# Seven products for batch 0's hidden layer, and four column strips for a pair's sums

## The chip, the cores and the metric

The kernel runs on one core of one Trainium2 chip. The metric is the time of one execution on the device in microseconds (us). The engines are named as the profile names them: PE is TensorE (PEld its weight loads, which overlap its products), DVE is VectorE, ACT is ScalarE, POOL is GpSimd and SP is SyncE, which here only issues transfers. Each engine works through its own list of instructions in order; they meet through semaphores.

## The reference, cut to what matters

Two blocks, one after the other, in float32. First an attention in which a query sees a key only if both fall in the same bucket of a six-bit hash; then a Fourier mixing block with a two-layer network.

```
B, H, S, D = 4, 8, 768, 64            # attention; DM = H*D = 512
mask   = bucket(q @ proj)[:, None] == bucket(k @ proj)[None, :]
scores = where(mask, q @ k.T / sqrt(D), -1e9)
attn   = exp(scores - max) / (sum + 1e-9)
x      = attn @ v                      # (B, S, DM)

mixed  = real(fft(fft(x, axis=1), axis=2))
u      = x + mixed
un     = (u - mean(u)) / sqrt(var(u) + 1e-6)
out    = u + relu(un @ w_ch1) @ w_ch2  # w_ch1: 512 x 2048, w_ch2: 2048 x 512
```

The two weights arrive as float64, and the kernel turns them into float32 on the chip.

## The kernel before, in words

**Attention.** A batch has four pairs of heads (`NPAIR`), numbered n = 4b + t. A pair is worked through in six key chunks of 128 keys (`NT`). `weigh` computes scores for the chunk (PE, line L869, and L862 for the five pairs 0 to 4, whose hash mask is added by a product), ACT takes the exponential (L873), and for the later pairs DVE applies the mask (L879, two instructions per chunk). DVE adds the chunk's weights to `acc` (L957). `values` multiplies the weights with v one chunk later (L890, tiles `oo`). The queue `pending` holds that later part. At the end of a pair, `scale` forms the sums of the weights over the keys by multiplying `acc` with ones (L910), writes them into two banks (one for each half of the queries), turns each by a DVE transpose (L914), adds a small number (L917), takes the reciprocal (L918), spreads it by a transpose back (L919) and multiplies x by it (L923). The ones are 64 columns wide, so that head h fills the partitions 64h to 64h+63. Two other products already write four strips of 32 partitions into one bank: the hash bits of pairs 5 to 15 (L804) and the weights' column sums in `average` (L656).

**Mixing.** `fold` and the tiles `cs`, `A`, `B` (L1007 to L1090) do the Fourier transforms as products with tables. The layer norm's mean is taken out of the weights beforehand (`average`, `centre`), and its factor is applied at the end. The hidden layer is `mlp0` for batch 0 and `mlp7` for batches 1 to 3. `mlp0` is the plain form: 16 blocks of 128 hidden units, two halves of the 768 columns, four products over the 512 inputs (L1314), 128 products of 128x128 with 384 columns in all, and one relu by ACT for each tile (L1318). `mlp7` takes two by two blocks with seven products instead of eight (Strassen's scheme in Winograd's form): per f of `HF` = 8 it issues 14 products (L1361), 112 in all, but has to add and subtract blocks: on the weights' side four combinations per f (`quarters`, L1149 to L1152, tile `tq`), which `mlp0` computes once beside its own work and writes to a scratch tensor `ad` in HBM with the plain blocks (L1154, L1155), on x's side four differences t1 to t4, and on the results' side five DVE additions (L1387, L1394, L1399, L1403, L1411), six ACT copies out of the product banks and four relus per f. The batches 1 to 3 read the blocks back from `ad` through a ring of 12 buffers. `outer7` is the second layer, in seven products for all batches (L1232); it is entered twice, once for each half of the hidden units, since the second weight's seven blocks for one half fill `w2` (tiles `right7`).

**The second weight's arrival.** `weights2` fetches 16 slices of w_ch2 as float64 through raw buffers in the tile `z` (L685, issued on POOL), and `narrow` converts each: DVE L631, L635 and L644 (twice), ACT L639, L646, L647. A slice can be fetched only when the slice that had its buffer has been converted. Three buffers are used. After each second slice, DVE forms four combinations (L1198 to L1201). The first eight slices are converted from the A and B steps of batch 0's mixing on, the other eight beside the second half of its hidden layer.

**Order.** The first attention, batch 0's, has an order written by hand for all engines (`manual_schedule`). From then on the mixing of batch b - 1 is interleaved with the attention of batch b: a loop draws steps of `mix` at an even rate over the 24 key chunks, counted by `MIX`, and a scheduler puts the instructions of each engine in order. The last mixing stands alone. Line numbers here are those of this kernel.

## Time and profile before

| | |
|---|---|
| median of 6 runs | 1111.39 us (1108.37 to 1113.9) |
| the profiled execution | 1111.44 us; span from first to last instruction 1109.7 us |
| PE busy | 1064.7 us of the span (96%) |
| DVE busy | 778.2 us (70%) |
| ACT busy | 455.9 us (41%) |
| batch 0's attention | 0 to 138 us |
| batch 1's attention with batch 0's mixing | 138 to 425 us |
| batch 2's attention with batch 1's mixing | 425 to 684 us |
| batch 3's attention with batch 2's mixing | 684 to 935 us |
| batch 3's mixing | 935 to 1110 us |

The bounds of the stages are the starts of each batch's `cs` products in the chain of waits. The stage of batch 0's mixing is the longest: 287 us, where the next has 259. A PE product in float32 is recorded as two instructions, so the counts of PE rows are twice the products. A PE row's busy time is the union of overlapping records; the mean of one is longer than its share.

### The profile page before, as it was taken

Reading aid. Unit: us, or ns where it says so; the run is one execution under the profiler, and the core shown is the slowest. Engines: PE = TensorE matmul, PEld = TensorE weight load, DVE = VectorE, ACT = ScalarE, POOL = GpSimd, SP = SyncE. Lnnn points to the kernel's source line nnn. Section 1 sums busy time; section 2 is a strip of 40 time slices with the busy share of each in tenths; the row PEclk is TensorE's granted clock in tenths of the full one; section 3 lists DMA queues with packets and bytes.
Section 4 is the critical chain, followed back from the end, with each engine's and each line's share of the span. In section 5 each row is a group of like instructions: output and inputs, shape, how many; then the busy total and the mean of one; then the engine's idle time right before and its main releaser. Section 6 shows DMA issues by size and latency. Waiting matters only on the chain.

```text
span 1109.7 us, 13908 instructions
## 1 busy us (share of the span) xinstructions
PE 1064.7 (96%) x4925; PEld 652.4 (59%) x4925; DVE 778.2 (70%) x1298; ACT 455.9 (41%) x879; POOL 79.2 (7%) x141
## 2 busy tenths in 40 slices
PE   7999987999999999999999999999999999999996
PEld 3334353555855676555664567545674569768675
DVE  5889968739598686975767796984866885644353
ACT  6778545525064224454325422355224422341420
POOL 1000000002110020030000011021000002100000
PEclk9999998999999999999999999999999999999998
DMA  9744444521057043222144234213032205122401
GB/s 228 200 95 114 82 152 118 209 46 27 1 141 226 22 116 123 48 67 77 29 152 91 67 67 166 37 45 94 17 114 67 76 29 171 48 87 77 132 19 41
DMA packets 175566, 103.13 MB, mean 93 GB/s; under 512 B 129408, under 2 KB 162816, under 8 KB 175488
## 3 DMA queue, kind: packets, MB, share of 16 engines
q1 hardware_dynamic: 168400, 83.93, 28.3%
q0 software_dynamic: 5520, 17.83, 5.1%
q8 instruction: 41, 0.67, 0.2%
q10 hardware_dynamic: 1568, 0.39, 0.2%
q14 instruction: 37, 0.30, 0.1%
HBM read 81.14 MB, written 20.97 MB: 92 GB/s over the span
## 4 chain that ended last, share of the span: by engine, by line
PE 68%; DVE 19%; DMA 4%; ACT 4%; issue 2%; SPq 1%; DVEq 0%; ACTq 0%
PE o L1232 23%; PE h_p L1361 18%; PE sc L869 7%; PE oo L890 6%; PE h L1314 6%; DVE acc L957 4%; DVE pk L879 3%; DMA zraw<-in_moe_w_ch_dram 3%; PE cs L1047 2%; PE sum L910 2%; PE A L1076 1%; ACT pk L873 1%; PE B L1076 1%; DMA ad<-tq 1%; DVE x L1090 1%
## 5 line engine op out<-in xcount | busy, mean ns | idle before, releaser
L1232 PE MATMUL o<-w,h 128*128 128x256 f32 x1152 | 258.9, 381 | 0.1
L1232 PEld LDWEIGHTS o<-w,h 128*128 128x128 f32 x1152 | 216.7, 190 | 42.6 <-issue 4.7
L873 ACT ACTIVATE pk<-sc 128x768 f32<-128x768 f32 x192 | 148.0, 808 | 89.9 <-PE sc L869 59.9
L879 DVE SCALAR_TENSOR_TENSOR pk<-qb,kb,pk 128x768 f32<-128x768 bf16 x132 | 128.5, 1011 | 62.2 <-ACT pk L873 61.5
L869 PE MATMUL sc<-qt,kt 64*128 64x384 f32 x768 | 154.6, 506 | 3.8 <-ACT pk L873 3.8
L890 PE MATMUL oo<-pk,vn 128*64 128x385 f32 (+1 forms) x768 | 151.8, 504 | 2.8 <-ACT x L903 2.5
L1361 PE MATMUL h_p<-x,w 128*128 128x384 f32 x384 | 139.0, 493 | 1.4 <-ACT h L1402 1.4
L1361 PE MATMUL h_p<-w 128*128 128x384 f32 x288 | 106.0, 491 | 0.7 <-ACT u L1103 0.7
L957 DVE TENSOR_TENSOR acc<-acc,pk 128x1536 f32<-128x1536 f32 (+1 forms) x72 | 105.6, 1480 | 0.6
L1361 PEld LDWEIGHTS h_p<-x,w 128*128 128x128 f32 x384 | 70.4, 190 | 57.7 <-ACT h L1402 5.1
L890 PEld LDWEIGHTS oo<-pk,vn 128*64 128x64 f32 x768 | 49.1, 137 | 93.7 <-issue 73.6
L869 PEld LDWEIGHTS sc<-qt,kt 64*128 64x128 f32 x768 | 67.0, 188 | 51.0 <-issue 25.4
L1314 PE MATMUL h<-x,w 128*128 128x384 f32 x256 | 86.2, 491 | 1.4 <-ACT h L1318 1.4
L1361 PEld LDWEIGHTS h_p<-w 128*128 128x128 f32 x288 | 53.3, 190 | 41.0 <-ACT w L1410 3.3
L1314 PEld LDWEIGHTS h<-x,w 128*128 128x128 f32 x256 | 47.6, 190 | 37.8 <-ACT h L1318 2.9
L1262 ACT COPY tq<-o 128x256 f32<-128x256 f32 x24 | 8.9, 372 | 115.4 <-PE o L1232 115.4
L1244 DVE SCALAR_TENSOR_TENSOR w<-o,rs,w 128x256 f32<-128x256 f32 x56 | 26.7, 478 | 40.8 <-PE o L1232 40.7
L1232 PE MATMUL o<-w 128*128 128x256 f32 x192 | 46.1, 383 | 4.0 <-DVE w L1244 2.4
L985 POOL DMA_DIRECT2D out_dram<-w x30 | 16.3, 546 | 428.0 <-issue 309.1
L1232 PEld LDWEIGHTS o<-w 128*128 128x128 f32 x192 | 35.9, 190 | 11.4 <-DVE w L1244 4.5
L1251 ACT COPY tq<-o 128x256 f32<-128x256 f32 x24 | 8.9, 370 | 74.6 <-PE o L1232 74.6
L1278 DVE TENSOR_TENSOR tq<-tq,o 128x256 f32<-128x256 f32 x24 | 10.1, 421 | 38.2 <-PE o L1232 38.2
(161 smaller groups left out, 1266.6 us busy)
## 6 DMA issues: line engine op xcount, KB each, us to landing
w<-ad SPq DMA_DIRECT2D x168, 128.0 KB, 2.0
w<-bd SPq DMA_DIRECT2D x42, 512.0 KB, 4.6
zraw<-in_moe_w_ch_dram POOLq DMA_DIRECT2D x21, 512.0 KB, 4.5
bd<-w SPq DMA_DIRECT2D x14, 512.0 KB, 4.9
vn<-in_v_dram SPq DMA_DIRECT2D x32, 192.0 KB, 3.5
qn<-in_q_dram SPq DMA_DIRECT2D x120, 48.0 KB, 2.3
kn<-in_k_dram SPq DMA_DIRECT2D x60, 96.0 KB, 3.3
ad<-tq SPq DMA_DIRECT2D x8, 512.0 KB, 4.1
```

Of the source, the lines that this page charges most:

```text
L869: last[0] = nc.tensor.matmul(ps[:, h, 0:HALF], kt[rows, ks], qt[rows, qs], start=kb is not None, stop=True,)
L873: nc.scalar.activation(pk[:, g, :, 0:HALF], ps[:, :, 0:HALF], AF.Exp, scale=SCALE)
L879: nc.vector.scalar_tensor_tensor(w, qb[:, h].rearrange("p (g s) -> p g s", g=2), kb[:, h, c : c + 1], w, op0=ALU.is_equal, op1=ALU.mult,)
L890: nc.tensor.matmul(oos[g][h * D : (h + 1) * D, 0:w], nat["v", n][:, (2 * c + h) * D : (2 * c + h + 1) * D], pk[:, g, h, 0:w], start=(c == ...
L910: nc.tensor.matmul(ps[h * D : (h + 1) * D, :], ones, part[:, g, h], start=(i == 0), stop=(i == len(sums) - 1),)
L957: nc.vector.tensor_tensor(acc[:, g], (first if c == 1 else acc)[:, g], new[:, g], op=ALU.add,)
L1047: nc.tensor.matmul(ps[:, pc + 2 * lo : pc + 2 * hi - 1 : 2], z[:, cp, pc, par, t * P : (t + 1) * P], ch[:, cp, pc, lo:hi], start=(cp == 0) ...
L1076: nc.tensor.matmul(ps[:, cols], F[:, par, k, t, j * P : (j + 1) * P], sq[:, t, k, cols], start=(t == 0), stop=(t == 1),)
L1232: nc.tensor.matmul(ps, a[:, r], right7[i][:, r], start=start and r == 0, stop=r == HF // 2 - 1, skip_group_check=not start,)
L1244: nc.vector.scalar_tensor_tensor(t[:, cols], src, r, t[:, cols], op0=ALU.mult, op1=ALU.add)
L1314: nc.tensor.matmul(ps, w1[:, c, fc * P : (fc + 1) * P], x[:, c, cols], start=(c == 0), stop=(c == NDC - 1),)
L1361: nc.tensor.matmul(ps, ring[n % NR][:, k], right[i][:, k], start=start and k == 0, stop=k == 1, skip_group_check=not start,)
```

## The change

Batch 0 takes its hidden layer by `mlp7` too, and `mlp0` is gone. It reads the weights' blocks from where they are: the plain ones from `w1`, the four combinations from `tq`, which `quarters(f + 1)` refills after the last product of f. The differences t1 and t2 of x lie in the buffer that `fold` uses for `ef`, and t4 in the third part of the tile `z`, so the arrival of w_ch2 has two raw buffers instead of three. The shared tag `t6` with two buffers becomes `acc` and `ef` with one each. One transposed tile row more is taken early (T = 3, 4, 5 ahead of the first products, 0, 1, 2 after the first half). In batch 1, `fold` starts a key chunk later.

In `scale`, the ones are 32 columns wide, and one bank takes all four combinations of query half and head, 32 partitions each. There is one transpose out of the bank, and `rc` has 12 columns instead of 24. Since the reciprocals of the two query halves now lie on different partitions, ACT moves them by eight copies of 32x12 into `rr`, from which DVE's transpose back reads. `scale` is cut in two at a yield: in batch 0 the second part (ACT's copies, DVE's transpose back and its product) follows a key chunk later, elsewhere it follows at once.

```diff
-    ones = const.tile([P, D], F32, tag="ones", name="ones")
+    ones = const.tile([P, 32], F32, tag="ones", name="ones")
...
+        ps = pt([P, HALF], f"sum{n}")
+        for i, part in enumerate(sums):
+            for j in range(4):
+                nc.tensor.matmul(
+                    ps[32 * j : 32 * j + 32, :], ones, part[:, j // 2, j % 2],
+                    start=(i == 0), stop=(i == len(sums) - 1),
+                )
         rt = wt([P, S], F32, "rt", f"rt{n}", 1)
+        nc.vector.transpose(rt[:, 0:HALF], ps)
+        rc = wt([P, HALF // 32], F32, "rc", f"rc{n}")
+        nc.vector.tensor_scalar(rc, rt[:, 0:HALF:32], S * EPS, None, op0=ALU.add)
+        nc.vector.reciprocal(rc, rc)
+        yield
+        rr = wt([P, 2, HALF // 32], F32, "rr", f"rr{n}")
         for g in range(2):
-            ps = pt([P, HALF], f"sum{n}_{g}")
-            for h in range(2):
-                for i, part in enumerate(sums):
-                    nc.tensor.matmul(
-                        ps[h * D : (h + 1) * D, :], ones, part[:, g, h],
-                        start=(i == 0), stop=(i == len(sums) - 1),
-                    )
-            nc.vector.transpose(rt[:, g * HALF : (g + 1) * HALF], ps)
-        rc = wt([P, S // 32], F32, "rc", f"rc{n}")
-        nc.vector.tensor_scalar(rc, rt[:, 0:S:32], S * EPS, None, op0=ALU.add)
-        nc.vector.reciprocal(rc, rc)
+            for i in range(4):
+                j = 2 * g + i // 2
+                nc.scalar.copy(rr[32 * i : 32 * i + 32, g], rc[32 * j : 32 * j + 32])
         nc.vector.transpose(
             rt.rearrange("p (j i) -> p j i", i=32),
-            rc[:, :, None].broadcast_to([P, S // 32, 32]),
+            rr.rearrange("p g j -> p (g j)")[:, :, None].broadcast_to([P, S // 32, 32]),
         )
...
-            acc = wt([P, 2, 2, HALF], F32, "t6", f"acc{n}", 2)
+            acc = wt([P, 2, 2, HALF], F32, "acc", f"acc{n}", 1)
...
+                for sc in scales:
+                    next(sc, None)
+                scales.clear()
                 while pending:
                     finish()
+                for sc in scales if b else ():
+                    next(sc, None)
                 pending.append((n, c, pk, oos, sums))
-                if c > 2:
+                if c > (3 if b == 1 else 2):
                     next(half, None)
...
-            ef = wt([P, 2, S], F32, "t6", f"ef{b}_{cp}_{pc}", 2)
+            ef = wt([P, 2, S], F32, "ef", f"ef{b}_{cp}_{pc}", 1)
...
-        yield from mlp0(b) if b == 0 else mlp7(b)
+        yield from mlp7(b)
...
-        arrival = Arrival(slices, [zt[:, i] for i in range(3)], NDC * DFF // WC)
+        arrival = Arrival(slices, [zt2[:, i] for i in range(2)], NDC * DFF // WC)
...
-    def mlp0(b):
...
+        if b == 0:
+            bt = wt([P, 2, S], F32, "ef", "bt", 1)
+            t1, t2, t4 = (
+                at.rearrange("p (k n) -> p k n", k=2)
+                for at in (bt[:, 0], bt[:, 1], zt2[:, 2, 0:S])
+            )
...
+            sd = [s1s[0].rearrange("p r n -> p (r n)")[:, 0:HALF]] * 2
...
+            quarters(0)
...
+            left = ring[n % NR]
+            if b == 0:
+                f = n // 7
+                if i >= S2:
+                    left = tq[:, i - S2].rearrange("p (k m) -> p k m", m=P)
+                else:
+                    c, r = (0 if i == A11 else 2), (f + HF if i == A22 else f)
+                    left = w1[:, c : c + 2, r * P : (r + 1) * P]
             for k in range(2):
                 nc.tensor.matmul(
-                    ps, ring[n % NR][:, k], right[i][:, k],
+                    ps, left[:, k], right[i][:, k],
...
+                if b == 0 and r < HF // 2 - 1:
+                    quarters(f + 1)
...
+        for half in range(2):
+            if b == 0 and half:
+                quarters(HF // 2)
+            for i, _ in enumerate(inner(half)):
+                if b == 0 and half and i % 4 < 3:
+                    next(arrival2, None)
+                yield
+            if b == 0 and half == 0:
+                for T in range(3):
+                    across(b, T, ut[T])
+            yield from outer7(b, half, hall, ut, rs, ss)
...
-    MIX = [2 + NT + NDC + 2 * (2 * HF + GT * 4)]
-    MIX += [2 + NT + NDC + 2 * (7 * HF // 4 + GT * 4)] * (B - 1)
+    MIX = 2 + NT + NDC + 2 * (7 * HF // 4 + GT * 4)
```

## The prediction

> **What bounds the kernel now.** I read the page's busy times first, then busy time by stage (the windows that front the table of stages), then the chain of waits inside batch 0's mixing, then the costliest groups for durations. The page:
>
> ```profile
> PE 1064.7 (96%) x4925; PEld 652.4 (59%) x4925; DVE 778.2 (70%) x1298; ACT 455.9 (41%) x879; POOL 79.2 (7%) x141
> ```
>
> PE is the bound, so PE work taken away counts, if nothing else takes its place. By stage (columns: stretch, length, busy time with instructions of PE, PEld, DVE, ACT, POOL; then granted clock, DMA share, GB/s):
>
> ```profile
> 0.00:138.30 138.30, 124.37 (x689) 53.77 (x689) 112.24 (x191) 95.27 (x166) 6.46 (x26) 0.99 0.61 144
> 138.30:195.90 57.60, 46.74 (x257) 27.80 (x255) 42.97 (x76) 28.16 (x54) 3.68 (x7) 0.94 0.45 130
> 195.90:250.10 54.20, 53.33 (x190) 27.93 (x192) 28.86 (x48) 22.17 (x43) 2.11 (x4) 1.00 0.40 130
> 250.10:323.50 73.40, 70.40 (x336) 46.65 (x333) 58.15 (x103) 27.38 (x53) 12.78 (x16) 1.00 0.16 37
> 323.50:376.30 52.80, 52.75 (x211) 26.81 (x212) 41.71 (x81) 24.04 (x46) 0.68 (x2) 1.00 0.52 161
> 424.90:683.90 259.00, 255.54 (x1187) 155.08 (x1185) 193.62 (x295) 102.48 (x198) 19.80 (x30) 1.00 0.31 82
> ```
>
> Lines two to five are batch 0's mixing: transforms (A), first half of h (B), second layer (C), second half of h (D). The last line is the same program part for batch 1. PE is busy 98% or more in B, D and the later stages. In A it idles 10.9 us and runs at a clock of 0.94. There the chain shows why: DVE waits for the write of `tq` to land, and later for a raw slice of w_ch2, and PE's clock falls (this stretch's eight `oo` products took 3.28 us, where 1.44 us is usual).
>
> ```profile
> 158.55 7.46 DMA ad<-tq
> 169.51 3.78 DMA zraw<-in_moe_w_ch_dram
> 179.89 4.86 DMA zraw<-in_moe_w_ch_dram
> 187.89 3.28 PE oo L890 x8
> 329.33 1.29 PE sum L910 x8
> 334.12 15.68 PE h L1314 x48
> 361.03 0.78 PE bits L804 x8
> ```
>
> **The change part by part.**
>
> *h's products.* 128 become 112. The chain's h row gives 15.68 / 48 = 0.327 us per instruction; 32 instructions fewer are 10.5 us of PE, half in B, half in D. With PE full there, that is a gain of 10.5 us before what follows.
>
> *h's other engines.* Per f, DVE gets five additions, and at the start four differences of 128x768; ACT gets six copies and four relus instead of four relus. From these rows of batches 1 to 3:
>
> ```profile
> L1387 DVE TENSOR_TENSOR h<-h 128x384 f32<-128x384 f32 x24 | 13.3, 554 | 23.1 <-ACT h L1386 23.1
> L1354 DVE TENSOR_TENSOR x<-x 128x768 f32<-128x768 f32 x3 | 2.9, 951 | 0.0
> L1383 ACT COPY h<-h_p 128x384 f32<-128x384 f32 x24 | 11.4, 477 | 10.4 <-PE h_p L1361 10.2
> L1318 ACT ACTIVATE h<-h 128x384 f32<-128x384 f32 x32 | 15.4, 486 | 46.7 <-PE h L1314 46.7
> ```
>
> DVE: 40 x 0.554 = 22.2 us and 4 x 0.95 = 3.8 us. ACT: 48 copies x 0.477 = 22.9 us more, relus about level. In A and B together DVE was busy 71.8 of 111.8 us; it becomes 71.8 + 3.8 + 11.1 = 86.7, against PE's 100.1 - 5.3 + 1.4 (three transposed tiles come here from C; batch 3's chain has such twelve `un` products in 1.45 us) = about 96. That fits, but B's beginning does not: the slices' conversions lie there. I charge 2 us. In D it does not fit: DVE goes from 41.7 to 52.8 us, PE from 52.75 to 47.5. D's floor becomes DVE's 52.8, so D gains nothing by itself; part of D's DVE work (masks, sums, `fold`) can slide into the second layer after it, where DVE is freer (37.2 of 48.6 us busy in 376.3 to 424.9). I take a charge of 4 of the 5.3 us. ACT has 46 of 52.8 us at most in D (24.0 + 11.5 + the copies below) and stays below PE. If these covers go, the whole 11 us of each half is exposed.
>
> *`quarters`.* Before, three sets were computed in a row in A, the second and third held DVE until `tq`'s transfer had landed (4.1 us median by the issue table):
>
> ```profile
> 154.48 0.43 DVE L1149 TENSOR_TENSOR tq<-w 128x256 f32<-128x256 f32 x1 [3.94 <-DMA ad<-tq]
> 166.03 0.42 DVE L1149 TENSOR_TENSOR tq<-w 128x256 f32<-128x256 f32 x1 [3.05 <-DMA ad<-tq]
> ```
>
> With one earlier wait of 0.95 us these are 7.9 us in which DVE stood. Now `quarters(f + 1)` needs S4's product of f done, and f's transfer has had f's 14 products (28 x 0.327 = 9.2 us and more) to land, so no transfer is waited for; the price is that the next f's second product follows two DVE additions (0.84 us), behind A11's product of 1.3 us: covered. The same transfers are issued on SP, later, in front of no attention load that is near its use. What is late next in A is DVE's own work and the raw slices. I book 5 of the 7.9 us.
>
> [...] By row, the stretch 180 to 200 us had 0.83 of the clock, 3.4 us lost. [...]
>
> *Two raw buffers.* A slice takes 0.53 us to issue, 4.5 us to land, and ACT 0.68 + 0.68 + 0.77 + 0.19 = 2.3 us: about 7.4 us for a round. Two buffers give a slice every 3.7 us at best, three every 2.5 us. Before, the first nine came in 58 us (fetches at 157.9 to 212.0), 6.4 us each, so engine order, not the buffers, mostly set the pace; yet ACT waited 28.3 us for slices in this stage. DVE or ACT waiting for a slice holds the mask and h's additions queued behind it, and PE behind those. From below 0 (slower drawing), from above one more round's difference, 2.5 us, for each of 12 later slices, 30 us. I take 3 us, near the row that shows the pace set elsewhere.
>
> *A pair's sums.* Eight instructions in two strips took 1.29 us; the same eight in four strips exist already as `bits`, L804, in 0.78 us: 0.5 us less. In batch 0, with 16 instructions, 2.65 becomes 0.78 + 0.66 = 1.44: 1.2 us less.
>
> ```profile
> 39.37 2.65 PE sum L910 x16
> L900 ACT COPY vs<-oo 128x1 f32<-128x1 f32 x16 | 2.5, 159 | 13.0 <-PE oo L890 13.0
> ```
>
> [...]
>
> DVE loses one transpose of 0.57 us per pair, but waits for ACT's eight copies. Nearest row L900: 0.16 us each, 1.3 us a pair, with two hand-overs about 1.6 us (from below 0.8 if they overlap, from above 8 x 0.37 = 3.0 by the 256-column copy). In the scheduled stages DVE's order puts the transpose back directly behind the reciprocal, so DVE stands about 1 us net per pair with the next masks queued behind it, and PE's `oo` behind those. DVE is at 75% there and PE holds other products: I book half, 0.5 us. Batches 2 and 3: 8 x (0.5 - 0.5) = 0, and I allow 1 us gain; batch 1: 0. In batch 0's attention the sums lie on the chain all four times: 4.8 us. ACT gets 5.2 us more in a stretch where it is busy 69%; three times a key chunk later, beside DVE's additions, but the exponential waits behind the copies; the fourth is exposed, 1.6 us. DVE saves 2.3 us. I book 2.5 us.
>
> *One `acc`.* The next pair's first addition must follow the sums' reading. Before, in batch 2 a pair's last sums end at 598.9 us and the next pair's first addition starts at 600.4; the four strips end earlier than the two. I take 0 (1 us a pair if PE draws the sums late). `fold` a chunk later: batch 1 only, hidden by the second layer.
>
> *The sum.* A and B: 5 + 5.3 - 2 = 8.3; D: 5.3 - 4 = 1.3; raw buffers -3; sums of batches 1 to 3: 1; batch 0's attention: 2.5; more even interleaving: 3, since 64 mixing steps instead of 68 stand against the same 24 chunks (A's remaining 5.9 us of idle halved). In all 13 us. Against the profiled execution's 1111.44 us this is 1098; that execution is the median of the runs (1111.39) within 0.1 us, so 1098 is also the forecast.
>
> **The rivals.** (1) *DVE is the bound of batch 0's mixing.* DVE was full from 304 to 357 us, and gets 11 us more per half: then h gains nothing, and A's gain is used up by the differences. What is left is the sums and A's waits: 3 to 8 us, 1105. For it: D's sum above. Against it: C's and the tail's free DVE time. (2) *The slices.* The mechanism ends slower: with two buffers, DVE stands at L631 or ACT at L639 for a landing in each round, everything queued behind. Price 30 us as above against 16 us of other gain: 1125. It decides from about 16 us of added waiting on PE's path. For it: landings of slices were 17.0 us of the chain of this stage up to h's second half (3.78, 4.86, 3.69 and 4.63 us). Against it: the pace of 6.4 us a slice before, well above the 3.7 us that two buffers allow. (3) *The strips do not gain*, since DVE stands behind ACT's copies and holds the masks: -8 us in batches 1 to 3, 1106.
>
> **How the numbers follow.** Forecast 1098 (1088 to 1104): 0.60. Rival 1, 1105: 0.15. Rival 3, 1106: 0.10, of which a part falls within no change. Rival 2, 1125: 0.11. More than forecast (A's clock and idle all regained, down to 1084): 0.04. Within 0.3%, 3.3 us, about what a measurement of this kernel can tell from no change, lies 1108 to 1114.7. Of rival 1 I count 0.04 there, of rival 3 another 0.04, the rest as faster: faster 0.81, within 0.3% 0.08, slower 0.11. The range of 1084 to 1112 leaves out rival 2 and little else; its lower end is A's 10.9 us of idle and 3.4 us of clock regained, its upper end rivals 1 and 3 with the unknown costs at their worse bounds.
>
> **What would show it.** Right: 224 instructions for batch 0's h instead of 256; no DVE wait on `ad<-tq`; sums x8 in about 0.8 us; DVE near 90% busy from 195 us to the second layer's end. Wrong: DVE or ACT waits on `zraw` beyond 40 us with PE idle beside them (rival 2); PE below 90% in B and D without such waits (rival 1); DVE waiting on L924's copies for over 1 us per pair with PE idle (rival 3).

## The result, and the profile after

The changed kernel takes 1106.08 us (median of 18 runs, 1104.1 to 1111.72), the kernel before beside it 1111.35 us (39 runs). The ratio is 0.9955, with a 95% interval of 0.9944 to 0.9966: 5 us faster, where 13 were forecast. The profiled execution took 1104.58 us, its span is 1102.7 us.

The page's busy times, to be held against those of before:

```profile
PE 1048.1 (95%) x4893; PEld 637.2 (58%) x4893; DVE 789.8 (72%) x1326; ACT 499.6 (45%) x1055; POOL 63.1 (6%) x141
```

PE is busy 16.6 us less, and the span is only 7.0 us shorter. PE now stands still for 9.6 us more than before, so a part of what PE was spared came back as waiting. Busy time by stage (columns as in the prediction's table; batch 0's attention, then A, B, C and D of its mixing; the last line is batch 1's mixing):

```profile
0.00:134.21 134.21, 117.01 (x689) 49.20 (x689) 108.79 (x183) 99.11 (x196) 6.44 (x26) 1.00 0.64 149
134.21:194.33 60.12, 50.13 (x276) 28.99 (x274) 45.80 (x80) 35.18 (x72) 3.15 (x6) 0.94 0.40 99
194.33:245.36 51.03, 48.12 (x164) 24.10 (x162) 39.72 (x71) 27.99 (x58) 2.11 (x4) 1.00 0.50 159
245.36:304.75 59.39, 56.97 (x287) 39.60 (x287) 44.27 (x76) 20.85 (x46) 7.58 (x13) 1.00 0.10 21
304.75:367.50 62.75, 58.47 (x235) 27.63 (x233) 58.37 (x113) 43.48 (x92) 2.63 (x5) 1.00 0.55 166
417.90:677.30 259.40, 255.54 (x1186) 154.32 (x1185) 190.56 (x291) 109.09 (x232) 13.56 (x29) 1.00 0.31 82
```

Batch 0's attention is 4.1 us shorter than its 138.3 us; 1.7 us of that is a half clock at 52 to 56 us in the profile before (0.52 and 0.63 granted in windows of 2 us), which this execution does not have. The stage of batch 0's mixing, from 134.2 to 417.9 us, lasts 283.7 us instead of 286.6. That is 2.9 us for the place where most of the forecast lay. The later stages are the same within 0.5 us. A is no shorter (60.1 us, where it was 57.6): PE idles 10.0 us in it, where it idled 10.9, and the clock is at 0.94 as before. The scheduler has moved instructions across the later seams, so B, C and D are compared by their shares: PE is busy 94% in B and 93% in D; before, with D cut at the same instruction (63.24 of 64.65 us), it was 98% in both. DVE is at 78% in B and at 93% in D.

What holds A is seen in the order of time (columns: start, duration, engine, line, operation, tiles; in brackets the idle time before it and what ended it):

```profile
176.47 0.53 POOL L685 DMA_DIRECT2D zraw<-in_moe_w_ch_dram  x1 [10.23 <-ACT zraw L647]
180.39 0.69 ACT L639 ACTIVATE zraw<-zraw 128x512 int32<-128x512 uint32 x1 [4.21 <-DMA zraw<-in_moe_w_ch_dram]
...
183.30 0.79 ACT L873 ACTIVATE pk<-sc 128x768 f32<-128x768 f32 x1
...
183.99 1.65 ACT L924 COPY rr<-rc 32x12 f32<-32x12 f32 x8
...
185.67 0.98 DVE L925 STREAM_TRANSPOSE rt<-rr 128x768 f32<-128x768 f32 x1 [1.28 <-ACT rr L924]
...
187.21 0.68 ACT L639 ACTIVATE zraw<-zraw 128x512 int32<-128x512 uint32 x1 [1.58 <-DMA zraw<-in_moe_w_ch_dram]
...
187.79 0.79 ACT L873 ACTIVATE pk<-sc 128x768 f32<-128x768 f32 x1
...
188.63 1.65 PE L869 MATMUL sc<-qt,kt 64*128 64x384 f32 x4 [2.99 <-ACT pk L873]
```

ACT's records show it taking its list in order: it stands 4.21 us for a slice, then converts it, then takes the exponential, then makes the eight copies, then stands 1.58 us for the next slice, and only then takes the exponential that frees the bank for PE's scores. PE stood 2.99 us. From 187.6 to 194.4 us, from inside that gap on, the granted clock is 0.50 (windows of 2 us, the granted clock is the third figure from the end):

```profile
186.00:188.00 2.00, 0.00 (x0) 0.00 (x0) 2.00 (x3) 0.79 (x2) 0.00 (x0) 0.90 0.03 10
188.00:190.00 2.00, 1.37 (x4) 0.50 (x4) 1.22 (x2) 1.77 (x3) 0.00 (x0) 0.50 0.00 0
190.00:192.00 2.00, 2.00 (x9) 1.43 (x9) 0.85 (x1) 1.67 (x3) 0.00 (x0) 0.50 0.00 0
192.00:194.00 2.00, 2.00 (x8) 0.68 (x4) 2.00 (x7) 0.41 (x2) 0.00 (x0) 0.50 0.00 0
194.00:196.00 2.00, 2.00 (x7) 1.08 (x6) 2.00 (x6) 1.28 (x3) 0.39 (x1) 0.90 0.00 0
```

Busy time times one minus the clock, summed over these rows, is 2.9 us of PE time lost, besides the gap. The kernel before had the same pair of losses at the same place, 2.9 us of clock by the same sum and a gap of 3.11 us:

```profile
186.24 1.65 PE L869 MATMUL sc<-qt,kt 64*128 64x384 f32 x4 [3.11 <-ACT pk L873]
```

Three groups of the strips (busy time and mean ns of one, then idle time before and what ended it), and the sums' row of before:

```profile
L924 ACT COPY rr<-rc 32x12 f32<-32x12 f32 x128 | 25.2, 197 | 13.9 <-DVE rc L918 9.4 <-DVE mt L1507 1.9 <-DVE mv L1125 1.3
L925 DVE STREAM_TRANSPOSE rt<-rr 128x768 f32<-128x768 f32 x16 | 15.6, 977 | 17.8 <-ACT rr L924 17.8
L908 PE MATMUL sum<-acc,ones 128*32 128x384 f32 x128 | 13.6, 498 | 0.4 <-DVE qkb L791 0.4
```

```profile
L910 PE MATMUL sum<-acc,ones 128*64 128x384 f32 x128 | 25.8, 492 | 0.4 <-DVE qkb L791 0.4
```

The sums are as cheap as forecast. But DVE stands 17.8 us for ACT's copies, 1.1 us in the mean pair.

### The profile page after: what moved, and what is told of

The parts are those of the page before. It is cut to its first block, busy times and chain, and to the rows that moved or that the text cites. A ratio compares the mean times of both kernels' runs of the same rounds, so it can differ in the third digit from the quotient of the medians.

```text
span 1102.7 us, 14065 instructions
## 1 busy us (share of the span) xinstructions
PE 1048.1 (95%) x4893; PEld 637.2 (58%) x4893; DVE 789.8 (72%) x1326; ACT 499.6 (45%) x1055; POOL 63.1 (6%) x141
## 4 chain that ended last, share of the span: by engine, by line
PE 57%; DVE 8%; ACT 3%; issue 1%; DMA 1%; DVEq 0%; ACTq 0%
PE o L1246 20%; PE h_p L1366 19%; PE oo L890 6%; PE sc L869 5%; PE cs L1062 2%; DVE pk L879 2%; PE A L1091 2%; PE B L1091 1%; DVE acc L964 1%; DMA zraw<-in_moe_w_ch_dram 1%; ACT rr L924 1%; DVE w L1258 1%; PE un L1117 1%; PE bits L804 1%; DVE h L1232 1%
## 5 line engine op out<-in xcount | busy, mean ns | idle before, releaser
L1366 PE MATMUL h_p<-x,w 128*128 128x384 f32 x448 | 163.1, 494 | 3.2 <-ACT h L1388 1.5
L890 PE MATMUL oo<-pk,vn 128*64 128x385 f32 (+1 forms) x768 | 154.9, 499 | 3.6 <-DVE pk L879 3.0
L879 DVE SCALAR_TENSOR_TENSOR pk<-qb,kb,pk 128x768 f32<-128x768 bf16 x132 | 128.9, 1012 | 29.3 <-ACT pk L873 29.1
L1366 PEld LDWEIGHTS h_p<-x,w 128*128 128x128 f32 x448 | 82.1, 190 | 70.7 <-ACT pk L873 5.4
L1246 PE MATMUL o<-w 128*128 128x256 f32 x176 | 42.3, 383 | 1.3 <-DVE w L1258 1.3
L1392 DVE TENSOR_TENSOR h<-h 128x384 f32<-128x384 f32 x32 | 17.8, 555 | 33.2 <-ACT h L1391 33.2
L1246 PEld LDWEIGHTS o<-w 128*128 128x128 f32 x176 | 32.8, 190 | 8.8 <-DVE w L1258 2.9
L1399 DVE TENSOR_TENSOR h<-h 128x384 f32<-128x384 f32 x32 | 17.7, 552 | 27.1 <-ACT h L1398 27.0
```

The source lines that it names most:

```text
L879: nc.vector.scalar_tensor_tensor(w, qb[:, h].rearrange("p (g s) -> p g s", g=2), kb[:, h, c : c + 1], w, op0=ALU.is_equal, op1=ALU.mult,)
L890: nc.tensor.matmul(oos[g][h * D : (h + 1) * D, 0:w], nat["v", n][:, (2 * c + h) * D : (2 * c + h + 1) * D], pk[:, g, h, 0:w], start=(c == ...
L1246: nc.tensor.matmul(ps, a[:, r], right7[i][:, r], start=start and r == 0, stop=r == HF // 2 - 1, skip_group_check=not start,)
L1366: nc.tensor.matmul(ps, left[:, k], right[i][:, k], start=start and k == 0, stop=k == 1, skip_group_check=not start,)
L1392: nc.vector.tensor_tensor(c21, c12, c21, op=ALU.add)
L1399: nc.vector.tensor_tensor(c22, c21, c22, op=ALU.add)
```

## The experiments

All ratios are to the kernel before. "Against the changed" is the difference of two ratios (0.9955 is the changed kernel's), times 1111.35 us; intervals of single ratios are 1 to 3 us either way, so differences below about 2 us say nothing.

The last column is the granted clock of TensorE, averaged over the span and over all runs of a kernel. A lower clock made the same products longer: at half the clock four instructions of the scores took 1.65 us (at 188.63 us), at the full clock 0.92 (at 177.12 us of fill_gap, below). Of two runs of the same kernel, the one with the lower clock tended to be the longer one: over 277 runs, 0.001 of clock went with 0.7 us. Taken over the whole span of 1105 us, 0.001 is 1.1 us. So I estimate a difference of 0.001 at 0.7 to 1.1 us.

| run | ratio, 95% interval | against before, us | against the changed, us | clock |
|---|---|---|---|---|
| the kernel before | 1 | | | 0.9945 |
| the changed kernel | 0.9955 [0.9944, 0.9966] | -5.0 | | 0.9926 |
| h7_only | 1.0001 [0.9986, 1.0015] | +0.1 | | 0.9928 |
| strips_only | 0.9977 [0.9962, 0.9991] | -2.6 | | 0.9922 |
| b_tq2 | 0.9981 [0.9968, 0.9995] | -2.1 | | 0.9953 |
| h8_split | 1.0015 [1.0003, 1.0028] | +1.7 | | 0.9942 |
| raw3 | 0.9969 [0.9957, 0.9981] | -3.4 | +1.6 | 0.9943 |
| fill_gap | 0.9930 [0.9911, 0.9949] | -7.8 | -2.8 | 0.9955 |
| late_slices | 0.9929 [0.9910, 0.9948] | -7.9 | -2.9 | 0.9927 |
| no_adds | 0.9914 [0.9896, 0.9932] | -9.6 | -4.6 | 0.9917 |
| no_adds_D | 0.9960 [0.9944, 0.9976] | -4.4 | +0.6 | 0.9911 |
| pool_adds | 0.9997 [0.9986, 1.0008] | -0.3 | +4.7 | 0.9919 |
| direct0 | 0.9985 [0.9971, 0.9998] | -1.7 | +3.3 | 0.9908 |
| no_copies | 0.9915 [0.9895, 0.9935] | -9.4 | -4.4 | 0.9878 |
| four_dve | 0.9911 [0.9898, 0.9924] | -9.9 | -4.9 | 0.9906 |
| strips_dve | 0.9906 [0.9889, 0.9922] | -10.4 | -5.4 | 0.9930 |
| dve_late | 0.9926 [0.9911, 0.9941] | -8.2 | -3.2 | 0.9897 |
| direct0_dve | 0.9928 [0.9908, 0.9948] | -8.0 | -3.0 | 0.9900 |
| direct_all_dve | 0.9926 [0.9902, 0.9950] | -8.2 | -3.2 | 0.9900 |
| dve_late_all | 0.9937 [0.9912, 0.9962] | -7.0 | -2.0 | 0.9900 |

### The parts of the change, each by itself

**h7_only**: the changed kernel with the end of a pair of before (ones 64 wide, two banks, no copies, no cut).

```diff
-        ps = pt([P, HALF], f"sum{n}")
...
+        for g in range(2):
+            ps = pt([P, HALF], f"sum{n}_{g}")
...
-                scales.append(scale(n, oos, sums))
-                next(scales[-1])
+                scale(n, oos, sums)
```

> The change without its strips: the sums, the ones and the end of a pair are those of before, all else is as changed. Theory M (the PE time that batch 0's seven products save comes back as PE waits on ACT and DVE, whatever the strips do): about 2 us below before, 1109. Rival C (ACT's eight copies per pair are what spoils it): the seven products show their full worth once the copies are gone, 9.5 us below before by the prediction's own steps, 1102.

Measured: no gain at all. Theory M was near, but 2 us too hopeful; rival C's 1102 is out. Where did 10.5 us of products go? First, h's own time on PE fell by less. Busy time of h's line alone over the first 420 us, before (L1314) and in this kernel (L1360):

```profile
0.00:420.00 420.00, 86.21 (x256) 0.99 0.46 120
```

```profile
0.00:420.00 420.00, 77.56 (x224) 0.98 0.47 123
```

That is 8.65 us and not 10.5: an instruction takes 0.346 us instead of 0.337. Groups of four that follow each other still start 1.29 us apart, 0.323 us per instruction; a group before other products takes 1.49 us until they start. So it is not the grouping in fours that costs, but that h's products are cut up more often by other products and by waits (PE stands 5.2 us ahead of them, 1.4 us before). And PE's busy time as a whole fell by only 2.9 us, from 1064.7 to 1061.8. Second, A's gap has become larger, with a longer half clock (0.50 from 180 to 188 us; 4.1 us of PE time are lost to it in the stage, reckoned as above, against 2.9):

```profile
179.44 1.65 PE L869 MATMUL sc<-qt,kt 64*128 64x384 f32 x4 [3.55 <-ACT pk L873]
```

Third, two sets of `oo` products take 2.35 us each instead of 1.51; no row of h shows this, and h8_split below makes it clear.

**strips_only**: the kernel before with the new `scale`, the ones 32 wide, and the cut (the whole diff of these functions).

> Before with the new end of a pair alone (strips, copies, and in batch 0 the second part a key chunk later). Theory M: 4 us from batch 0's attention and about nothing elsewhere, 1107.5. Rival C: the copies cost more in the later batches than the strips bring, 1111 to 1115. The prediction's steps: 2.5 + 1, 1108.

Measured: 2.6 us below before, a little short of both M's and the prediction's numbers. The two parts together give 5.0 us, each by itself 2.6 and nothing. The intervals of 0.9955 and 0.9977 just overlap, so the seven products are worth 0 to 2.4 us.

**h8_split**: before with the buffers of the change alone.

```diff
-            acc = wt([P, 2, 2, HALF], F32, "t6", f"acc{n}", 2)
+            acc = wt([P, 2, 2, HALF], F32, "acc", f"acc{n}", 1)
...
-            ef = wt([P, 2, S], F32, "t6", f"ef{b}_{cp}_{pc}", 2)
+            ef = wt([P, 2, S], F32, "ef", f"ef{b}_{cp}_{pc}", 1)
...
-                if c > 2:
+                if c > (3 if b == 1 else 2):
...
-        pwf = wt([P, 2, P], F32, "t6", "pwf", 2)
+        pwf = wt([P, 2, P], F32, "ef", "pwf", 1)
```

> Before with the third, quiet part of the change alone: the shared tag t6 of two buffers becomes acc and ef with one each, and fold starts a key chunk later in batch 1. The prediction booked 0: 1111.4. Rival B (one acc holds the next pair's first addition back, one ef holds fold's second half behind the first half's last reading, and the seven products alone therefore show no gain): 1114 or more, which would be the place where a part of h's 10.5 us went.

Measured: 1.7 us slower (0.3 to 3.1), less than rival B's 2.6 and not the 0 that was booked. The timeline shows where, once each in batches 2 and 3: a set of `oo` products, with its weight loads. In before, in h8_split, and in the changed kernel:

```profile
855.65 1.51 PE L890 MATMUL oo<-pk,vn 128*64 128x385 f32 x8
```

```profile
481.57 2.34 PE L890 MATMUL oo<-pk,vn 128*64 128x385 f32 x8
481.57 0.19 PEld L890 LDWEIGHTS oo<-pk,vn 128*64 128x64 f32 x2 [0.55 <-DVE pk L879]
482.41 0.20 PEld L890 LDWEIGHTS oo<-pk,vn 128*64 128x64 f32 x4 [0.65 <-DVE pk L879]
```

```profile
474.93 2.90 PE L890 MATMUL oo<-pk,vn 128*64 128x385 f32 x8
...
476.32 0.19 PEld L890 LDWEIGHTS oo<-pk,vn 128*64 128x64 f32 x2 [0.56 <-DVE pk L879]
...
734.29 2.90 PE L890 MATMUL oo<-pk,vn 128*64 128x385 f32 x8
```

In these stages of before each such set takes 1.51 us: the two heads write different 64-column halves, and their products start within 0.01 us of each other. In the slow sets the second head's first product starts 0.84 us (h8_split) or 1.40 us (changed kernel) after the first head's, each time 0.05 to 0.06 us after DVE has finished that head's mask (L879). So the price is a wait for a late mask. PE counts as busy all the while with the first head's products, and only the weight loads show the wait (0.65 us of PEld in h8_split, 0.56 in the changed kernel). Twice 0.83 us in h8_split is as much as its 1.7 us. The changed kernel has two sets of 2.90 us and a third of 2.43 (at 674.88 us): 3.7 us. Why the masks come later with these buffers stays open.

**b_tq2**: before with a second buffer for the weights' combinations (`QB` is the size of one block in `w2`).

```diff
+    w2f = w2.rearrange("p c f -> p (c f)")
...
         st = tq[:, 0:4].rearrange("p i (k m) -> p i k m", m=P)
+        if f % 2:
+            st = w2f[:, 7 * QB :].rearrange("p (i k m) -> p i k m", i=4, m=P)
```

> Before with a second buffer for the four combinations of the weights (every second set lies in the part of w2 that is free then), so that DVE need not wait for tq's transfer. It takes the 7.9 us of DVE waits out of A without any other part of the change. The prediction booked 5 us of them: 1106.4. Theory M (those waits lay beside PE's waits on ACT and are not on the path): 1111.

Measured: 2.1 us (0.6 to 3.6). So the 7.9 us in which DVE stood for `tq`'s transfer were partly on the path, and less than the 5 us booked. No DVE wait for this transfer is left; of the copies in w2 one waits a little:

```profile
L1154 DVE TENSOR_TENSOR w<-w 128x256 f32<-128x256 f32 x4 | 1.7, 421 | 0.8 <-DMA ad<-w 0.8
```

### What takes the seven products' gain

**raw3**: three raw buffers.

```diff
-        arrival = Arrival(slices, [zt2[:, i] for i in range(2)], NDC * DFF // WC)
+        arrival = Arrival(slices, [zt2[:, i] for i in range(3)], NDC * DFF // WC)
...
-                for at in (bt[:, 0], bt[:, 1], zt2[:, 2, 0:S])
+                for at in (bt[:, 0], bt[:, 1], bt[:, 1])
```

> The changed kernel with three raw buffers for w_ch2 instead of two; for the room, t4 overwrites t2, so that the product A22 and the product S2 read one tile (wrong values, the same number of instructions on every engine, and t4's difference waits for S2's reading or the other way round only at the beginning). Theory M with the prediction's price: 3 us below the changed kernel, 1103. Rival S (the slices are what ate the gain): 7 us or more below, 1099 or less. Nothing at all, 1106, if engine order sets the pace of the slices as before.

Measured: no gain; it is 1.6 us on the slower side, within the intervals. ACT's waits for slices are no shorter in its profile (25.0 us). The count of buffers is not what makes slices late. The prediction's other rival is answered by a row of the waits between 134 and 418 us (total, times, longest), in before and in the changed kernel:

```profile
ACT zraw L639 <- DMA zraw<-in_moe_w_ch_dram: 28.3, 14, 4.8
```

```profile
ACT zraw L639 <- DMA zraw<-in_moe_w_ch_dram: 20.5, 13, 4.2
```

**fill_gap**: eight idle products ahead of the scores that wait at 188.6 us. They lie in oo's bank and disturb that pair's values.

```diff
+            if n == 5 and c == 3 and g == 1:
+                with behind():
+                    for _ in range(8):
+                        last[0] = nc.tensor.matmul(
+                            spot[0][0:D, 400:512], ident[:, 0:D], ident[:, 0:112],
+                            start=True, stop=True, skip_group_check=True,
+                        )
...
+            spot[0] = oos[0]
```

> The changed kernel with eight idle products (ident by ident, 112 columns, into unused columns of oo) put into PE's list just ahead of the scores that wait for ACT at 188.6 us, so that PE is not still for 3 us there; the order of everything else is the same but for five of the un transposes, which come after those scores. Theory G (the gap costs its length and then 3.4 us of half clock, in every version so far): the half clock goes, 2 to 3.4 us below the changed kernel, 1103 to 1104. Rival (the clock falls for another reason, or the time after the gap is set by DVE and ACT): 1106, and a granted clock of 0.5 in the same place.

Measured: 2.8 us below the changed kernel, with about 2 us of uncertainty either way. Its profiled execution shows a half clock in the same place still, but a shorter one, and shows what the length of a gap does not decide:

```profile
177.12 0.92 PE L876 MATMUL sc<-qt,kt 64*128 64x384 f32 x4 [3.30 <-ACT pk L880]
...
191.93 0.94 PE L876 MATMUL sc<-qt,kt 64*128 64x384 f32 x4 [2.04 <-ACT pk L880]
```

```profile
176.00:178.00 2.00, 0.88 (x4) 0.30 (x4) 0.90 (x1) 2.00 (x5) 0.00 (x0) 1.00 0.00 0
178.00:180.00 2.00, 0.90 (x4) 0.19 (x2) 2.00 (x6) 1.30 (x3) 0.37 (x1) 1.00 0.00 0
...
190.00:192.00 2.00, 0.07 (x2) 0.07 (x2) 2.00 (x3) 1.49 (x3) 0.00 (x0) 1.00 0.00 0
192.00:194.00 2.00, 2.00 (x9) 1.15 (x9) 2.00 (x6) 1.67 (x3) 0.00 (x0) 0.67 0.00 0
194.00:196.00 2.00, 2.00 (x7) 1.19 (x8) 2.00 (x6) 1.97 (x4) 0.00 (x0) 0.50 0.04 8
```

A gap of 3.30 us left the clock whole, one of 2.04 us halved it for some 3.4 us: 1.7 us lost instead of 2.9. Over all its runs the clock is 0.9955 against the changed kernel's 0.9926, by the estimate above 2.0 to 3.2 us, which is the whole gain. So theory G holds in direction (less idling there, less half clock, less time), and its sentence on the gap's length does not.

**late_slices**: the first slices four mixing steps later.

```diff
-        other = after(2 + NT, other, islice(arrival2, HF + 1))
+        other = after(2 + NT + NDC, other, islice(arrival2, HF + 1))
```

> The changed kernel with the first half of w_ch2's slices drawn from the end of the transforms on (four mixing steps later), so that in A neither ACT nor DVE stands for a slice. Theory M/G (the 3 us gap with its half clock in A comes from ACT standing 4.2 us behind a slice, and what is moved into B has room there): 3 to 6 us below, 1100 to 1103. Rival S (the slices are short of time everywhere: nine slices in B's 51 us, beside h's additions, hold PE there instead): 1106 or above.

Measured: 2.9 us below the changed kernel, just short of M's 3 to 6. When the slices come matters; that more may be under way brings nothing. Whether the gain is the clock's is not shown: the profiled execution has no half clock in A, but over all runs the clock is that of the changed kernel.

**no_adds** and **no_adds_D**: without DVE's five additions per f in batch 0, in both halves or in the second alone.

```diff
-                nc.vector.tensor_tensor(c21, c12, c21, op=ALU.add)
+                if b:
+                    nc.vector.tensor_tensor(c21, c12, c21, op=ALU.add)
...
```

In no_adds_D the condition is `b or half == 0`.

> The changed kernel without the five DVE additions per f of batch 0's hidden layer (40 in all, 22 us of DVE; ACT's copies and relus and the products stay), so its values are wrong. Theory D, the prediction's first rival (DVE is the bound of batch 0's mixing): 8 us below the changed kernel or more, 1098. Theory M (the saved time is lost at a few places where ACT stands in its order behind a slice or a copy): 3 us or less, 1103 to 1106.

> The changed kernel without the five DVE additions per f in the second half of batch 0's hidden layer alone (20 of the 40, beside the slices' second half). The prediction charged D with 4 us for DVE and B with 2: then most of the 4.6 us of leaving all out comes from here, 3 us or more below the changed kernel, 1103. If B is where they cost, 1 us or less, 1105 to 1106.

Measured: 4.6 us for all, nothing for those of D. The 4.6 lie between D's 8 and M's 3, and the pair turns the prediction's placing round: the additions cost in the first half (by difference; they were not taken out there alone), where DVE is at 78%, and not in D, where it is at 93%. The clock of no_adds_D is lower than the changed kernel's, which may hide a gain of 1.0 to 1.7 us (estimate); that is still little. The shares of busy time did not say which engine binds here.

**pool_adds**: two of the five on POOL.

```diff
-                nc.vector.tensor_tensor(c22, c21, c22, op=ALU.add)
+                (nc.vector if b else nc.gpsimd).tensor_tensor(c22, c21, c22, op=ALU.add)
...
-                nc.vector.tensor_tensor(c21, c21, sd[1], op=ALU.add)
+                (nc.vector if b else nc.gpsimd).tensor_tensor(c21, c21, sd[1], op=ALU.add)
```

> The changed kernel with two of the five additions per f of batch 0's hidden layer on POOL instead of DVE (c22 = c21 + c22 and the last, c21 + sd). Leaving all five out brought 4.6 us. If DVE's load is the cause, two fifths of it, 1.8 us below, 1104.3, or a little less for POOL's slower additions. If the cause is the chain of additions itself (product, copy, addition, relu, and then the next f's copy into the same tile), a slower POOL makes it longer: 1107 to 1110.

Measured: 4.7 us slower. POOL takes 1.9 to 2.6 times as long as DVE for the same addition (a row that stays on DVE stands below the two of POOL), and PE's waits for ACT's first copy of an f, `h_p <- h L1388`, grow from 1.5 us in the changed kernel to 6.7 us. The longer chain costs more than the lighter DVE brings (1.8 us was the hope).

```profile
L1399 POOL TENSOR_TENSOR h<-h 128x384 f32<-128x384 f32 x8 | 11.4, 1421 | 46.4 <-ACT h L1398 46.4
L1416 POOL TENSOR_TENSOR h<-h,w 128x384 f32<-128x384 f32 x8 | 8.3, 1043 | 33.6 <-ACT w L1415 26.6 <-DVE w L644 6.7 <-DVE h L1408 0.3
L1392 DVE TENSOR_TENSOR h<-h 128x384 f32<-128x384 f32 x32 | 17.8, 555 | 36.3 <-ACT h L1391 36.2
```

**direct0**: batch 0's additions out of the banks.

```diff
-                nc.scalar.copy(c21, p6)
-                nc.vector.tensor_tensor(c21, c12, c21, op=ALU.add)
+                if b == 0:
+                    nc.vector.tensor_tensor(c21, c12, p6, op=ALU.add)
+                else:
+                    nc.scalar.copy(c21, p6)
+                    nc.vector.tensor_tensor(c21, c12, c21, op=ALU.add)
...
```

The same is done with p5 and p7, twice each.

> The changed kernel, but in batch 0 the five additions per f read the product from its bank instead of from ACT's copy (40 ACT copies of 0.48 us fewer; DVE as before, since its additions out of a bank take 0.49 to 0.55 us as well). Theory K (the chain product, ACT copy, DVE addition, ACT relu is what holds PE: the wait for ACT is the longest in it): 4 us or more below the changed kernel, 1102. Theory D (DVE's load): no gain or less than 1.5 us, 1105 to 1107; banks held until a late DVE has read them would make it slower, 1110.

Measured: 3.3 us slower. Theory K falls: with 19 us of ACT's copies gone the kernel is not faster, and ACT's 48 copies of h are not what eats the gain. An estimated 1.2 to 2.0 of the 3.3 us go with the lower clock, 0.9908. The additions are no dearer than before (0.54 to 0.55 us). PE's waits in this stage are at the same places as in the changed kernel, with the second grown from 2.2 us and the third from 1.5:

```profile
PE sc L869 <- ACT pk L873: 4.6, 3, 3.0
PE kb L828 <- ACT qb L531: 3.8, 1, 3.8
...
PE h_p L1366 <- ACT h L1388: 2.4, 1, 2.4
PE h_p L1366 <- DVE h L1392: 1.7, 1, 1.7
```

The last row is new: PE now waits 1.7 us for DVE to release a bank. These products have two banks in this stage (`ps_1`); in the changed kernel ACT's copies release them, and PE has no wait for DVE's L1392 there. That is the rival's clause in the expectation.

### The copies

**no_copies**: without them; DVE takes 24 columns of the transposed sums and transposes back at once.

```diff
-        nc.vector.tensor_scalar(rc, rt[:, 0:HALF:32], S * EPS, None, op0=ALU.add)
+        nc.vector.tensor_scalar(rc, rt[:, 0:HALF:16], 1.0, None, op0=ALU.add)
...
-                nc.scalar.copy(rr[32 * i : 32 * i + 32, g], rc[32 * j : 32 * j + 32])
...
```

**four_dve**: four by DVE, done so that four of the eight fall away.

```diff
-                    ps[32 * j : 32 * j + 32, :], ones, part[:, j // 2, j % 2],
+                    ps[32 * j : 32 * j + 32, :], ones, part[:, j % 2, j // 2],
...
-        nc.vector.reciprocal(rc, rc)
+        rr = wt([P, 2, HALF // 32], F32, "rr", f"rr{n}")
+        nc.vector.reciprocal(rr, rc[:, None, :].broadcast_to([P, 2, HALF // 32]))
         yield
-        rr = wt([P, 2, HALF // 32], F32, "rr", f"rr{n}")
-        for g in range(2):
-            for i in range(4):
-                j = 2 * g + i // 2
-                nc.scalar.copy(rr[32 * i : 32 * i + 32, g], rc[32 * j : 32 * j + 32])
+        for i in range(4):
+            j, g = i ^ 1, 1 - i % 2
+            nc.vector.tensor_copy(rr[32 * i : 32 * i + 32, g], rr[32 * j : 32 * j + 32, g])
```

> The changed kernel without ACT's eight copies per pair: DVE takes 24 columns of the transposed sums (two of each block of 32, wrong values) as the kernel before did, adds 1 instead of the small number, and transposes back at once. Theory C (DVE standing behind the copies is the loss; 17.8 us of such waits are in the trace): 6 us or more below the changed kernel, 1100. Theory M: the copies matter where ACT or DVE is late anyway, batch 0's mixing above all: 2 to 3 us, 1103.5. The prediction's own price: 1.6 us once in batch 0 and 0.5 per later pair, 7.6 us, 1098.5.

> The changed kernel with the spreading of the reciprocals mended: the strips are ordered so that each lies beside the one it is exchanged with, DVE's reciprocal writes both halves at once, and four copies of 32x12 by DVE itself exchange the rest, instead of eight by ACT. Theory C+M (it is the hand-over to an ACT that is late, more than the copying, that costs; leaving the copies out brought 4.4 us): 3 us or more below the changed kernel, 1103 or less; DVE gets about 4 x 0.17 = 0.7 us per pair but no longer waits for ACT. Rival (DVE has no room, each of its instructions counts): 1105 to 1107.

Measured: 4.4 us for leaving them out, between M and C, and 4.9 us for letting DVE make four, as theory C+M expected. The two are one within the intervals (2.6 us), so most of the price was the hand-over to ACT and back. That DVE's own copies cost nothing is not shown: no_copies has the lowest clock of all, 0.9878, against 0.9906, and by the estimate it would be 1.9 to 3.1 us the faster at an equal clock. In four_dve the wait of 17.8 us is gone:

```profile
L924 DVE STREAM_TRANSPOSE rt<-rr 128x768 f32<-128x768 f32 x16 | 15.6, 975 | 0.4
...
L923 DVE COPY rr<-rr 32x12 f32<-32x12 f32 x64 | 10.7, 167 | 1.2
```

DVE is busy 11 us more with copies, and stands 17 us less.

**strips_dve**: the same four copies in strips_only, so eight products in batch 0.

> Before (eight products in batch 0) with the strips and the four DVE copies. Theory M (the seven products come into their own only where ACT is not late): the seven products are worth 4 us or more here, so this stands at 1106.5 or above, against four_dve's 1101.5 in the same measure. Rival (their work on DVE and ACT eats the products whatever the end of a pair does): they are worth 0 to 2 us here too, and this stands at 1101.5 to 1103.5.

Measured: 10.4 us below before, the lowest ratio of all, though four_dve and others lie within its interval. The rival holds: with the end of a pair mended, the seven products are worth -0.6 us (0.9906 against 0.9911), with 2.3 us either way. Part of it is the clock, 0.9930 without them and 0.9906 with them, by the estimate 1.6 to 2.6 us. At an equal clock they would be worth 1 to 2 us. Against strips_only the mended copies bring 7.9 us.

**dve_late**, **direct0_dve**, **direct_all_dve** and **dve_late_all** are four_dve with another edit each: late_slices, direct0, the additions out of the banks in all batches, and the second part of a pair's end a key chunk later in all batches. The last one's edit:

```diff
-                for sc in scales if b else ():
-                    next(sc, None)
```

> The changed kernel with the four DVE copies and with the first slices of w_ch2 drawn four mixing steps later. If the two losses are apart in place, the gains add up: 2.9 + 3 us, 1100. If both are one and the same place in A (ACT late for the scores, the 3 us gap and its half clock), the sum is that of the larger: 1103.

> direct0 together with the four DVE copies in place of ACT's eight. If ACT's lateness is one cause for both, less than the sum of the two gains; if they are apart, the sum: with 4 us for the one and 4.9 for the other, 1097.

> As direct0_dve, with the additions out of the banks in all four batches. Theory K: another 1 to 3 us below direct0_dve, mostly in the last mixing, which stands alone. Rival (the copies free the banks early, and that is why they are there; two banks for h cannot wait for DVE): slower than direct0_dve by 3 us or more.

> four_dve with the second part of a pair's end a key chunk later in all batches, not in batch 0 alone. If DVE's masks still stand behind the end of a pair in the later batches, 1 to 3 us below four_dve, 1099; if four_dve left nothing there, the same, 1101.5; slower, 1103 to 1105, where x's row is late for the next fold or the next pair's oo.

Measured: 0.9926, 0.9928, 0.9926 and 0.9937, none below four_dve's 0.9911 and all with intervals that touch it or come near. late_slices' 2.9 us does not add to the copies' 4.9. That fits with one place that both heal, ACT late in A, but it is not shown: these four kernels also have low clocks (0.9897 to 0.9900). dve_late_all lies on the slower side, as the last case of its expectation has it, within the intervals. In direct_all_dve neither theory K's further gain nor the rival's loss is seen.

## Why the prediction was wrong, and where it was right

**A and B, 8.3 us booked, and D, 1.3.** This is the step that failed. Batch 0's seven products with all that belongs to them were booked at 9.6 us net, with the buffers' 3 off and the interleaving's 3 on; measured are nothing alone (h7_only, 1.6 us either way), 2.4 us beside the strips, -0.6 beside the mended strips. The booking took what PE and DVE were spared as time saved. The terms as measured leave 3.3 us of it, and some 3 us more were lost for which no cause was found. Term by term:

- the products, 10.5: 8.65 on PE in h's own line, since they are cut up by other products and by waits.
- `tq`'s waits, 5: 2.1 when they alone are removed. A's idle time with the whole change is 10.0 us after 10.9. The waits lay beside ACT's, and when they went ACT was late next: the slices and the copies.
- DVE's additions, 6 charged over B and D: 4.6 in all, but in the first half, none in D.
- one `acc` and one `ef`, 0: 1.7 in h8_split, 3.7 in the changed kernel's three slow sets of oo. The argument (the next pair's first addition comes late enough) looked at DVE's addition. The price came through DVE's masks, for which the second head's products start 0.84 to 1.40 us late, and shows as PE's busy time.
- the clock, 0 (the sum has no term for it): in the profiled executions this stage loses 2.9 us before and after. Over all runs 0 is not right: the clock fell from 0.9945 to 0.9926, by the estimate 1.3 to 2.1 us. The gap with its clock costs 5.9 us in the changed kernel (2.99 + 2.9), and h7_only's 7.7 (3.55 + 4.1).
- more even interleaving, 3: nothing shows it. It rested on half of A's idle time going away, and A's idle time did not.

Together: of the 9.6 booked, 1.9 are missing at the products, 2.9 at `tq`, 1.7 at the masks, 1.2 at h7_only's longer half clock in A and 3 at the interleaving; the additions give back 1.4 and the raw buffers 3. That makes 3.3 us; measured is 0 with 1.6 either way. So about 3 us of the loss stay open. The additions and the buffers were measured in the changed kernel and not in h7_only, and terms measured one by one need not add.

As forecast, h takes 224 instructions (the row above), and no wait of DVE for `tq`'s transfer is left. DVE near 90% busy from 195 us on did not come: it is 82% over B, C and D.

**Two raw buffers, 3 us.** Wrong in size: a third buffer brings nothing. The pace of 6.4 us for a slice, which the prediction read as set by engine order, was the better sign (nine fetches in 54.1 us are eight steps of 6.8 us; the reading stays). Rival 2 is out. Its 30 us also took 2.5 us for a slice, where its own two paces, 3.7 and 2.5 us, differ by 1.2. ACT's 46 us in D do not come out of their terms either: 24.0 + 11.5 leave 10.5 us for the copies, where a pair was given 3.0 at most. Neither slip decided the forecast.

**The strips, 1 us in batches 1 to 3 and 2.5 in batch 0.** Right in mechanism and near in size. Sums take 0.85 us in batch 1, and the full worth is 10.4 us (strips_dve), where the prediction's 1.2 us for each pair of batch 0 and 0.5 for each of the 12 others give 4.8 + 6 = 10.8. The 0.66 us for eight further instructions in the 1.2 was an estimate, which no row of before shows; in the changed kernel the second eight of a pair in batch 0 start 0.67 us after the first, and all sixteen take 1.50 us, where 1.44 was booked:

```profile
38.60 0.85 PE L908 MATMUL sum<-acc,ones 128*32 128x384 f32 x8
39.27 0.83 PE L908 MATMUL sum<-pk,ones 128*32 128x384 f32 x8
```

ACT's copies eat 7.9 us of the full worth in the kernel with eight products and 4.9 with seven; the prediction's terms for them, 1.6 us once and 0.5 us for each of 12 later pairs, give 7.6. What is left, 2.6 us (strips_only), stands beside the 3.5 booked. So the 0.5 us for the exposed wait came out about right, though no row stood behind the half that it took because PE "holds other products".

**Rival 3** (DVE stands behind ACT's copies, -8 us) had the sign that the profile shows at once, over 1 us of DVE wait per pair, but not the size: 8 us off the strips' 3.5 would leave strips_only slower than before, and it is 2.6 us faster. That its 1106 is the time measured is luck; the loss against the forecast lies in the seven products.

**Rival 1** named DVE as the bound. Its mark, PE below 90% in B and D, did not come (94% and 93%), and emptying DVE in D brought nothing. In the chain DVE does hold nearly the whole stretch from 364.7 to 388.1 us, at D's end and after it, up to the copies of a pair's end:

```profile
387.91 0.15 DVE rc L918
...
388.08 0.20 ACT rr L924
...
389.77 0.38 ACT tq L1265
...
390.20 1.99 PE o L1246 x8
```

PE's second layer waits here for ACT's evacuation, which stands behind the eight copies: 1.7 us on the chain in one pair.

## What to carry to other kernels

Small instructions that waited for another engine held up the queue behind them here: sixteen sets of eight tiny copies on a half-idle ACT cost 5 to 8 us, with 17.8 us of DVE's waits, and with four on the fuller DVE, which need no hand-over, most of that came back. Fewer instructions on the bound engine were a gain only in part: 32 fewer, booked at 10.5 us, took 8.65 us off their own line and nothing off the time (h7_only). So price the chain, and where an experiment can take a wait away alone, do so before booking it in full. Look at a group's duration too, not only at PE's idle time: where one of two products that run side by side was late, the group took 2.90 us instead of 1.51, and the wait looked like work. And compare the clock of all runs before a difference of 2 us is given to an edit: between runs of one kernel, 0.001 of clock went with 0.7 us.

## What the runs showed of the hardware that was not expected

- The granted clock fell to 0.50 for 3.4 us (before, at 52 us), 6.8 us (before and the changed kernel, in A) and 10.2 us (h7_only, in A), reckoned from windows of 2 us. The gap before it does not decide by its length alone: in fill_gap's profiled execution 3.30 us went without loss, and 2.04 us with 1.7 us of PE time lost. What decides is not shown.
- Four products into two 64-column halves, eight instructions, took 1.51 us where the halves were used side by side (before, at 855.65 us), and 2.90 us where first one half and then the other was used (the changed kernel, at 474.93 us). By their records, neighbours on different halves started within 0.01 us, and on the same half 0.32 us or more apart.
- An addition of 128x384 in float32 took 1.04 to 1.42 us on POOL and 0.55 us on DVE (pool_adds); a 32x12 copy 0.20 us on ACT (the changed kernel) and 0.17 us on DVE (four_dve).
